# Top-k attention and two MLPs on one core: first head's keys and scores ahead of the rest, 64-token products with high and low words side by side, output chunks in pairs

## The chip, the cores and the metric

The kernel runs on one core of one Trainium2 chip. The metric is the device time in microseconds (us) of one execution, and the kernel's time is the median over its runs. One more execution is recorded by the hardware profiler; its span runs from the first instruction to the last. PE is TensorE (matmuls), PEld its weight loads, DVE VectorE, ACT ScalarE, POOL GpSimd, SP the engine that issues most DMAs.

## The reference, cut to what matters

```python
# q, k, v: 4 x 8 heads x 576 tokens x 64
scores = q @ k.T / sqrt(64)
kth    = the 32nd largest score of each row
attn   = softmax(scores where scores >= kth, else -1e9)
x      = (attn @ v), heads side by side           # 2304 tokens x 512
x      = (relu(x @ w_in) ** 2) @ w_out            # 512 -> 2048 -> 512
h      = x @ w2_in
out    = max(0.01 * h, h) @ w2_out
```

Everything is float32. The weights of the two MLPs reach the device as 64-bit words and are turned into two float32 parts there.

## The kernel before, in words

**Units and tiles.** The 2304 tokens are cut into nine units (`UNITS`: a batch, a first token, and 256, 320 or 64 tokens), and two heads form a head pair, so each unit has four. One head pair of one unit (a `uh` in the code) is cut into tiles of 128 rows of scores by 576 keys; the first tiles of the first `uh` belong to its first head, the next ones to its second. Two tiles form a pair. Only one unit has 64 tokens; its four head pairs make eight products of 64 tokens each.

**High and low words.** A float32 value is held as a rounded part (type float32r) and the remainder, so that a product becomes a few fast float32r products. `split_k` makes the two for one head's keys (the rounded part on ACT or POOL, the remainder on DVE for the first head pair), `split_q` for the queries. A score tile is made in two halves of 288 keys by `scores`: two matmuls, then an ACT copy to SBUF (L312).

**Top-k on DVE.** For each tile DVE runs four MAX8 (L929) and three MATCH_REPLACE8 (L931), written out slot by slot in the loop at the end; a pair of tiles has 16 slots. ACT then forms the exponentials, PE transposes them, and `av` or `av_split` multiplies with V. In `av_split` (L448) the transposed weights lie in `PTs` as four blocks of high words (0 to 3), four of low words (4 to 7) and one of leftover keys; nine matmuls of n columns add up in one PSUM bank. The two halves of the partitions are then added (ACT L453 copies one half, DVE L454 adds it to `xf`), and `x_out` splits the sum into `xh` (ACT L469) and `xl` (POOL L473). `xf` and `tmp` have one buffer each.

**MLP.** Token blocks of 512, 256, 384, 512, 256 and 384 go through the two MLPs as soon as their attention output is complete (`moe`, matmuls at L656, L693, L695). Each layer adds up in up to four PSUM banks (`acc`). After the second layer ACT copies each bank to an SBUF tile `y` (L714) and sends it out (L716). `y` is a 128 x 1024 tile of the tag `wc`, which has two buffers, and one chunk of 512 columns takes one such tile.

**What sets the order.** `at(slot, fn)` puts each step into a slot; the slots run in order, so the slot is a step's place in program order. Slots below zero lie ahead of the first MAX8. A scheduler then orders each engine's queue by that order and by planned times; `urgent` and `high_priority` move a step ahead in it, and `behind(key)` (`tc.issue_after`) places a step after a named instruction. `cur["rate"]` sets how many MLP pieces are put between the slots. Score tiles of the batches in `EARLY` are computed ahead by PE (slots 2 to 222) and stored in DRAM. On each engine the queue is worked in order.

Of the kernel before, what the change touches and what calls it, by code (L numbers as in the profile page):

```python
# [58 lines left out]
WCB = 2  # L59
# [29 lines left out]
def topk_attention_moe_moe2_kernel(  # L89
# [28 lines left out]
    def bank():  # L118
        return psum.tile([P, 512], F, tag="att", name="att", bufs=3)
# [4 lines left out]
    def behind(key):  # L124

        return tc.issue_after(cur[key].ins) if key in cur else ExitStack()

    def split_hi(dst, src, act=False):
        if act:
            ACT.activation(dst, src, AF.Copy)  # L130
            return
        POOL.tensor_scalar(dst, src, 1.0, 1.0, op0=OP.mult, op1=OP.mult)
# [84 lines left out]
    def at(slot, fn, *a):  # L217
        events.setdefault(slot, []).append((fn, a))
# [10 lines left out]
    def load_k(b, hp, st):  # L229
        if b in EARLY:  # L230
            KT[b, hp] = ahead.tile([P, 2, S], R, tag="KTa", name="KTa", bufs=KPB)
        else:
            KT[b, hp] = pool.tile([P, 2, S], R, tag="KT", name="KT", bufs=4)
        x = ahead if b in EARLY else pool
        st["k"] = x.tile([P, 2, S], F, tag="kraw", name="kraw", bufs=1 if b in EARLY else KRB)
        SP.dma_start(st["k"], k[b, hp])

    VT = {}
    vdram = {}
# [29 lines left out]

    def split_k(b, hp, st, h):  # L270
        raw, kt = st["k"][:, h], KT[b, hp][:, h]
        split_hi(kt, raw, st["i"] < 2)
        (DVE if (st["i"], h) in KLO_D else POOL).tensor_tensor(kt[64:128], raw[64:128], kt.bitcast(F)[64:128], op=OP.subtract)

    def load_q(uh):
# [6 lines left out]
    def split_q(uh, c):  # L282
        q1, q2 = uh["qs"]
        n = uh["n"]
        for h, o in ((0, W - 64 - n), (1, 64)):
            d1, d2, x = q1[:, h, o:o + n], q2[:, h, o:o + n], uh["q"][:, h, 0:n]
            if c == 0:
                split_hi(d1, x, uh["idx"] in HI_SET)
            else:
                (DVE if uh["idx"] in QLO_D else POOL).tensor_tensor(d2, x, d1.bitcast(F), op=OP.subtract)  # L290


    def scores(t, half):
        uh = t["uh"]
        d = uh["qs"]
        kt = KT[uh["b"], uh["hp"]]
        if half == 0:
            if direct(uh) and not kept(uh):
                t["s"] = sbufs[t["i"] % NS]
            else:  # L300
                t["s"] = ahead.tile([P, S], F, tag="stage", name="stage", bufs=NST)
        ks = slice(half * HALF, (half + 1) * HALF)
        mm = [(x[:, h, c:c + P], kt[:, h, ks]) for h, c in t["parts"] for x in d]
        if not direct(uh):
            ps = stage_psum.tile([P, 512], F, tag="sp", name="sp", bufs=SPB)
        elif t["i"] // 2 <= first_done + 1 or kept(uh):
            ps = stage_psum.tile([P, 512], F, tag="sd", name="sd", bufs=SDB)
        else:
            ps = bank()
        for i, (l, r) in enumerate(mm):  # L310
            PE.matmul(ps[:, 0:HALF], lhsT=l, rhs=r, start=i == 0, stop=i == len(mm) - 1)  # L311
        ACT.activation(t["s"][:, ks], ps[:, 0:HALF], AF.Copy, scale=0.125)  # L312
        if half == 1 and (kept(uh) or not direct(uh)):
            t["sd"] = dram.tile([P, S], F, tag=f"sd{t['i']}", name=f"sd{t['i']}")
            SP.dma_start(t["sd"], t["s"])
# [124 lines left out]
    def av_split(uh, h):  # L440
        n = uh["n"]
        c = slice(uh["c0"] + h * n, uh["c0"] + h * n + n)
        vt, pts = VT[uh["b"], uh["hp"]][0], late["PT"]
        ps = bank()[:, 0:n]
        mm = [(vt[:, h, j, :], pts[:, x + j, c]) for j in range(NJ) for x in (0, 4)]
        mm.append((vt[:, h, 4, :], pts[:, 8, c]))
        for i, (l, r) in enumerate(mm):
            PE.matmul(ps, lhsT=l, rhs=r, start=i == 0, stop=i == len(mm) - 1)  # L448
        if h == 0:
            uh["xf"] = late["pool"].tile([P, 320], F, tag="xf", name="xf", bufs=1)  # L450
            uh["tmp"] = late["pool"].tile([P, 320], F, tag="tmp", name="tmp", bufs=1)
        mine, other = slice(h * 64, h * 64 + 64), slice(64 - h * 64, 128 - h * 64)
        ACT.activation(uh["tmp"][mine, 0:n], ps[other], AF.Copy)  # L453
        DVE.tensor_tensor(uh["xf"][mine, 0:n], ps[mine], uh["tmp"][mine, 0:n], op=OP.add)  # L454

    def x_out(uh, hs):
        g0, n, hp = uh["u"]["g0"], uh["n"], uh["hp"]
# [169 lines left out]
    def moe(j, layer):  # L627
# [75 lines left out]
        for c in range(na):  # L703
            if layer == 0:
                xh, xl = x[c]
                with tc.high_priority(offset=SEAM):
                    ACT.activation(xh[:, 0:n], acc[c][:, 0:n], AF.Copy)
                    DVE.tensor_tensor(xl[:, 0:n], acc[c][:, 0:n], xh.bitcast(F)[:, 0:n], op=OP.subtract)
            else:
                if j == len(blocks) - 1:  # L710
                    y = sbufs[c][:, 0:512]
                else:
                    y = pool.tile([P, 1024], F, tag="wc", name="y", bufs=WCB)[:, 0:512]
                ACT.activation(y, acc[c], AF.Copy)  # L714
                for p0, n0, r0 in rows(blk["g0"] + c * P, P):
                    ACT.dma_start(out[r0:r0 + n0, :], y[p0:p0 + n0])  # L716
# [13 lines left out]
    for uh in in_time + [uh for uh in uhs if not direct(uh)]:  # L730
        b, hp, i = uh["b"], uh["hp"], uh.get("di")
        z = uh["zs"]
        if uh["first"] and direct(uh):
            st = {"i": i}
            st["n"] = len(order)
            order.append(b)
            z0 = after(z - 62, ("kraw", st["n"] - KRB), *[("KT", x, hp) for x in range(b)])
            at(z0, load_k, b, hp, st)
            for h in range(2):
                at(z0 + 12 * h + 11, split_k, b, hp, st, h)  # L740
            used["kraw", st["n"]] = z0 + 23
            assert z0 + 24 <= z
        if (b, hp) not in vdone or split(uh) and VTB < NHP:
            vdone.add((b, hp))
            zv = score_slot(uh["ti"]) + DLEAD + 4
            if split(uh):
                zv = max(zv, opened)
            at(zv, load_v, uh)
            if split(uh):
                at(zv + 6, split_v, uh, 0)  # L750
                at(zv + 9, split_v, uh, 1)
        if not direct(uh):
            continue
        uh["qs"] = qsets[i % 2]
        z0 = after(z - 70, ("qraw", i - 2))
        z1 = max(after(z - 20, ("q", i - 2)), z0 + 6)
        assert z1 + 4 <= z
        at(z0, load_q, uh)
        at(z1, split_q, uh, 0)
        at(z1 + 4, split_q, uh, 1)  # L760
        used["qraw", i] = z1 + 4
        used["q", i] = used["KT", b, hp] = (z if kept(uh) else score_slot(uh["last"])) + 2
# [48 lines left out]
    for p in range(NPAIRS):  # L811
        pr = dict(t=tiles[2 * p:2 * p + 2], p=p)
        pairs.append(pr)
        z = 16 * p
        if p == first_done:
            assert all(direct(t["uh"]) and not split(t["uh"]) for t in pr["t"])
            for i, t in enumerate(pr["t"]):
                at(z - DLEAD + 5 * i, scores, t, 0)
                at(z - DLEAD + 2 + 5 * i, scores, t, 1)
            at(z + 13, urgent(shifts), pr)  # L820
            for i in range(2):
                at(z + 13, urgent(drop), pr, i)
                at(z + 13, urgent(expo_sum), pr, i)
            at(z + 13, urgent(recip), pr)
            for i in range(2):
                at(z + 14, urgent(pt_main), pr["t"][i])
            at(z + 14, urgent(pt_left), pr)
            continue
        for i, t in enumerate(pr["t"]):
            if kept(t["uh"]):  # L830
                at(t["uh"]["zs"], scores, t, 0)
                at(t["uh"]["zs"] + 2, scores, t, 1)
            if kept(t["uh"]) or not direct(t["uh"]):
                at(z - LEAD + i, load_s, t)
            else:
                at(z - DLEAD + 5 * i, scores, t, 0)
                at(z - DLEAD + 2 + 5 * i, scores, t, 1)
            if i == 0:
                at(z + 14, shifts, pr)
            at(z + 14 + i, drop, pr, i)  # L840
            at(z + 16 + i, expo_sum, pr, i)
            if split(t["uh"]):
                at(z + 20 + i, norm, pr, i)
            at(max(z + 20 + 3 * i, z + 21 + i), pt_main, t)
        at(z + 18, recip, pr)
        at(z + 26, pt_left, pr)
# [160 lines left out]
```

## Time and profile before

| | |
|---|---|
| median of 3 runs | 1196.27 us (1195.66 to 1200.34) |
| profiled execution, its own time | 1196.31 us |
| its span | 1194.4 us |
| PE busy | 1126.8 us, 94% |
| DVE busy | 863.5 us, 72% |
| ACT busy | 804.7 us, 67% |
| POOL busy | 753.7 us, 63% |
| mean granted TensorE clock | 0.986 |

An engine's share is a mean over stages: DVE is nearly always busy while there is attention to do, up to about 900 us, and hardly afterwards; PE is busy nearly throughout from about 190 us on, when the first MLP begins.

### The profile page before, as it was taken

To read this page: it belongs to the slowest core of one execution; us is meant where nothing else is said; L and a number is where in the kernel's file an instruction comes from. 1 tells how busy PE (TensorE), PEld (TensorE's weight loads), DVE (VectorE), ACT (ScalarE), POOL (GpSimd) and SP (SyncE) were. 2 spreads that over 40 slices of the span, in tenths; PEclk is the share of its full clock that TensorE was granted. 3 is DMA by queue.
4 is the path that set the end of the run, shared out by engine and by line. 5 is a ranking of instruction groups with operands and counts; after the bars stand their busy time and mean duration, and the time that the engine had idled before them with its cause. 6 is when DMAs were issued, how large, how long until landed. Compare 5 with 4: busy or idle time off the path is not lost.

```text
span 1194.4 us, 20043 instructions
## 1 busy us (share of the span) xinstructions
PE 1126.8 (94%) x6376; PEld 987.6 (83%) x6376; DVE 863.5 (72%) x1797; ACT 804.7 (67%) x1785; POOL 753.7 (63%) x968
## 2 busy tenths in 40 slices
PE   5899978989899999899999999999999999999998
PEld 4777756768688889888999898788888899999997
DVE  7999998987878879999999999999991000110011
ACT  6999887998889878767777776766765233333322
POOL 7968747999878757867899675777755233002100
PEclk9899989999899999999999999999999999999999
DMA  9868766999899578899889888777665589779974
GB/s 313 273 213 292 242 229 233 333 356 329 296 311 316 211 234 297 298 360 392 300 315 323 276 303 273 266 228 219 212 211 159 170 317 346 252 249 346 358 251 135
DMA packets 108200, 329.53 MB, mean 276 GB/s; under 512 B 17216, under 2 KB 25408, under 8 KB 104000
## 3 DMA queue, kind: packets, MB, share of 16 engines
q1 hardware_dynamic: 105472, 323.53, 79.0%
q10 hardware_dynamic: 2624, 4.72, 1.1%
q8 instruction: 52, 0.85, 0.3%
q14 instruction: 52, 0.43, 0.1%
HBM read 257.03 MB, written 71.17 MB: 275 GB/s over the span
## 4 chain that ended last, share of the span: by engine, by line
PE 64%; DVE 6%; ACT 3%; POOL 3%; issue 1%; DMA 1%; ACTq 0%; POOLq 0%
PE h L656 28%; PE acc L695 15%; PE acc L693 13%; PE att L448 4%; DVE m L929 3%; PE att L351 3%; DVE w L931 2%; PE att L311 1%; DMA out_dram<-y 1%; POOL gl L676 1%; PE att L366 1%; ACT PTs L356 0%; POOL wo L568 0%; POOL wi L568 0%; ACT whole L358 0%
## 5 line engine op out<-in xcount | busy, mean ns | idle before, releaser
L656 PE MATMUL h<-xh,wi 128*128 128x512 f32 (+2 forms) x1280 | 345.0, 344 | 2.9 <-ACT ga L673 1.1
L929 DVE MAX8 m<-w 128x8 f32<-128x576 f32 x432 | 313.1, 748 | 2.6
L676 POOL TENSOR_TENSOR gl<-ga,gh 128x512 fp32r<-128x512 f32 (+2 forms) x160 | 163.2, 1022 | 143.4 <-ACT gh L675 116.5
L656 PEld LDWEIGHTS h<-xh,wi 128*128 128x128 f32 x1280 | 226.2, 190 | 27.7 <-ACT ga L666 2.1
L931 DVE MATCH_REPLACE8 w<-m,w 128x576 f32<-128x576 f32 x288 | 213.1, 742 | 0.7
L656 PE MATMUL h<-xl,wi 128*128 128x512 f32 (+2 forms) x640 | 204.5, 339 | 0.0
L359 POOL TENSOR_TENSOR PTs<-whole,PTs 128x512 fp32r<-128x512 f32 x112 | 145.4, 1303 | 42.6 <-ACT whole L358 42.2
L693 PE MATMUL acc<-gh,wo 128*128 128x512 f32 (+2 forms) x768 | 156.5, 342 | 4.9 <-ACT y L714 3.6
L695 PE MATMUL acc<-wo,gh 128*128 128x512 f32 x576 | 153.2, 397 | 2.0 <-ACT gh L675 2.0
L693 PEld LDWEIGHTS acc<-gh,wo 128*128 128x128 f32 x768 | 126.9, 190 | 18.0 <-ACT y L714 4.6
L330 ACT ACTIVATE e<-s,m 128x576 f32<-128x576 f32 x144 | 111.0, 784 | 26.0 <-DVE m L929 21.4
L656 PEld LDWEIGHTS h<-xl,wi 128*128 128x128 f32 x640 | 120.0, 189 | 10.2
L676 DVE TENSOR_TENSOR gl<-ga,gh 128x384 fp32r<-128x384 f32 x32 | 17.9, 559 | 151.2 <-ACT gh L675 150.7
L673 ACT ACTIVATE ga<-h 128x512 f32<-128x512 f32 (+2 forms) x96 | 46.5, 490 | 119.6 <-PE h L656 116.3
L695 PEld LDWEIGHTS acc<-wo,gh 128*128 128x128 f32 x576 | 105.5, 188 | 22.5 <-ACT gh L675 2.2
L929 DVE MAX8 m<-s 128x8 f32<-128x576 f32 x144 | 104.6, 747 | 20.5 <-ACT s L312 19.1
L334 ACT ACTIVATE e<-e,nb 128x576 f32<-128x576 f32 x144 | 111.6, 780 | 5.0 <-POOL nb L324 4.6
L931 DVE MATCH_REPLACE8 w<-m,s 128x576 f32<-128x576 f32 x144 | 106.6, 743 | 0.4
L351 PE MATMUL att<-ident,e 128*128 128x128 f32 x576 | 90.9, 279 | 7.8 <-ACT e L334 4.5
L693 PE MATMUL acc<-gl,wo 128*128 128x512 f32 (+2 forms) x384 | 88.7, 351 | 7.6 <-POOL gl L676 7.6
L346 POOL TENSOR_SCALAR e<-e,rc 128x576 f32<-128x576 f32 x112 | 83.7, 760 | 16.7 <-DVE rc L342 13.0
L668 POOL TENSOR_TENSOR ga<-ga 128x512 f32<-128x512 f32 (+2 forms) x80 | 67.0, 838 | 41.1 <-ACT gh L667 40.4
(100 smaller groups left out, 2080.7 us busy)
## 6 DMA issues: line engine op xcount, KB each, us to landing
wi<-wd SPq DMA_DIRECT2D x160, 512.0 KB, 5.5
wo<-wd SPq DMA_DIRECT2D x160, 512.0 KB, 5.3
wraw<-in_w_dram SPq DMA_DIRECT2D x32, 1024.0 KB, 7.5
sd<-stage SPq DMA_DIRECT2D x76, 288.0 KB, 3.0
s<-sd SPq DMA_DIRECT2D x76, 288.0 KB, 5.4
wd<-wi SPq DMA_DIRECT2D x32, 512.0 KB, 6.7
wd<-wo SPq DMA_DIRECT2D x32, 512.0 KB, 6.7
vd<-VT SPq DMA_DIRECT2D x16, 640.0 KB, 6.5
```

The lines of the kernel that those rows point to most:

```text
L330: ACT.activation(t["e"], t["s"], AF.Prelu, bias=pr["m8"][:, i, 31:32], scale=-1.0, alpha=1.0 / FAR)
L334: ACT.activation(e, e, AF.Exp, bias=pr["nb"][:, i:i + 1], scale=-FAR, accum_out=pr["sum"][:, i:i + 1])
L346: POOL.tensor_scalar(e, e, pr["rc"][:, i:i + 1], 1.0, op0=OP.mult, op1=OP.mult)
L351: PE.transpose(ps[:, j * P:(j + 1) * P], t["e"][:, j * P:(j + 1) * P], ident)
L359: POOL.tensor_tensor(pts[:, 4:8, c:c + P], whole, pts.bitcast(F)[:, 0:4, c:c + P], op=OP.subtract)
L656: PE.matmul(two[r][:, 0:n], lhsT=ws[r][:, w, c * P:(c + 1) * P], rhs=x[c][y][:, 0:n], start=cnt == mine[0], stop=cnt == mine[-1])
L668: POOL.tensor_tensor(a[:, 0:n], a[:, 0:n], a[:, 0:n], op=OP.mult)
L676: (DVE if j >= GLD else POOL).tensor_tensor(gl[:, 0:n], a[:, 0:n], gh.bitcast(F)[:, 0:n], op=OP.subtract)
L693: PE.matmul(acc[c][:, 0:n], lhsT=wo[:, w, cs], rhs=g[:, 0:n], start=first, stop=last)
L695: PE.matmul(acc[c], lhsT=g[:, cs], rhs=wo[:, w, :], start=first, stop=last)
L929: cur["dve"] = DVE.max(out=m8[:, x, 8 * r:8 * r + 8], in_=t["s"] if r == 0 else t["w"])
L931: cur["dve"] = DVE.match_replace(out=t["w"], in_to_replace=m8[:, x, 8 * r:8 * r + 8], in_values=t["s"] if r == 0 else t["w"], imm_value=NEG)
```

## The change

Five edits, with no change to the constants:

1. The keys of the first head pair are loaded in two halves: the first head's ahead of everything, then the first queries, then the second head's keys. The second head's split waits (`behind("opened")`) until the second score tile has been copied, and moves from slot -69 to slot -22.
2. The split of the second queries (`di == 1`) is also placed behind that copy.
3. The scores of the first pair of tiles are `urgent`.
4. A 64-token product takes a high and a low block together: the moving operand is 128 columns wide, there are four such matmuls and one of 64 columns in place of nine of 64. The copy and the add (L453, L454) become 128 wide, and a POOL add joins the two halves.
5. Two output chunks share one `wc` tile.

Since the raw keys have one buffer (`KRB = 1`), the later slot of the first head pair's last split also moves the loads of the following head pairs' keys to later slots (the second from -60 to -21).

```diff
-        SP.dma_start(st["k"], k[b, hp])
+        if st["i"]:
+            SP.dma_start(st["k"], k[b, hp])
+        else:
+            SP.dma_start(st["k"][:, 0], k[b, hp][:, 0])
+
+    def load_k_rest(b, hp, st):
+        SP.dma_start(st["k"][:, 1], k[b, hp][:, 1])
...
-        split_hi(kt, raw, st["i"] < 2)
+        with behind("opened") if st["i"] == 0 else ExitStack():
+            split_hi(kt, raw, st["i"] < 2)
...
-                split_hi(d1, x, uh["idx"] in HI_SET)
+                with behind("opened") if uh.get("di") == 1 else ExitStack():
+                    split_hi(d1, x, uh["idx"] in HI_SET)
...
-        ACT.activation(t["s"][:, ks], ps[:, 0:HALF], AF.Copy, scale=0.125)
+        out = ACT.activation(t["s"][:, ks], ps[:, 0:HALF], AF.Copy, scale=0.125)
+        if t["i"] == 1:
+            cur["opened"] = out
...
-        ps = bank()[:, 0:n]
-        mm = [(vt[:, h, j, :], pts[:, x + j, c]) for j in range(NJ) for x in (0, 4)]
+        m = 2 * n if n == 64 else n
+        ps = bank()[:, 0:m]
+        if n == 64:
+            mm = [(vt[:, h, j, :], pts[:, j:j + 5:4, c]) for j in range(NJ)]
+        else:
+            mm = [(vt[:, h, j, :], pts[:, x + j, c]) for j in range(NJ) for x in (0, 4)]
         mm.append((vt[:, h, 4, :], pts[:, 8, c]))
         for i, (l, r) in enumerate(mm):
-            PE.matmul(ps, lhsT=l, rhs=r, start=i == 0, stop=i == len(mm) - 1)
+            PE.matmul(ps[:, 0:n] if i == len(mm) - 1 else ps, lhsT=l, rhs=r, start=i == 0, stop=i == len(mm) - 1)
...
-        ACT.activation(uh["tmp"][mine, 0:n], ps[other], AF.Copy)
-        DVE.tensor_tensor(uh["xf"][mine, 0:n], ps[mine], uh["tmp"][mine, 0:n], op=OP.add)
+        xf, tmp = uh["xf"], uh["tmp"]
+        ACT.activation(tmp[mine, 0:m], ps[other], AF.Copy)
+        DVE.tensor_tensor(xf[mine, 0:m], ps[mine], tmp[mine, 0:m], op=OP.add)
+        if n == 64:
+            POOL.tensor_tensor(xf[mine, 0:n], xf[mine, 0:n], xf[mine, n:m], op=OP.add)
...
-                    y = pool.tile([P, 1024], F, tag="wc", name="y", bufs=WCB)[:, 0:512]
+                    if c % 2 == 0:
+                        both = pool.tile([P, 2, 512], F, tag="wc", name="y", bufs=WCB)
+                    y = both[:, c % 2]
...
             at(z0, load_k, b, hp, st)
+            if i == 0:
+                at(z0 + 6, load_k_rest, b, hp, st)
             for h in range(2):
-                at(z0 + 12 * h + 11, split_k, b, hp, st, h)
-            used["kraw", st["n"]] = z0 + 23
-            assert z0 + 24 <= z
+                at(-22 if i == 0 and h == 1 else z0 + 12 * h + 11, split_k, b, hp, st, h)
+            used["kraw", st["n"]] = -22 if i == 0 else z0 + 23
+            assert z0 + 23 <= z
...
-        at(z0, load_q, uh)
+        at(z0 if i else z0 + 12, load_q, uh)
...
-                at(z - DLEAD + 5 * i, scores, t, 0)
-                at(z - DLEAD + 2 + 5 * i, scores, t, 1)
+                mine = urgent(scores) if p == 0 else scores
+                at(z - DLEAD + 5 * i, mine, t, 0)
+                at(z - DLEAD + 2 + 5 * i, mine, t, 1)
```

## Rows read from the trace of the kernel before

**Rows 1.** Page, busy time of each engine: us, share of the span, instructions.
```profile
PE 1126.8 (94%) x6376; PEld 987.6 (83%) x6376; DVE 863.5 (72%) x1797; ACT 804.7 (67%) x1785; POOL 753.7 (63%) x968
```

**Rows 2.** Windows: stretch in us, its length, then each engine's busy time.
```profile
20.00:60.00 40.00, 33.71 (x190) 27.90 (x189) 40.00 (x87) 37.72 (x104) 34.87 (x51) 0.91 0.86 302
...
500.00:560.00 60.00, 57.88 (x406) 52.81 (x407) 59.13 (x134) 42.53 (x107) 44.45 (x68) 1.00 0.94 349
560.00:960.00 400.00, 395.96 (x2133) 348.55 (x2132) 336.46 (x729) 265.84 (x559) 280.74 (x348) 1.00 0.76 253
960.00:1194.00 234.00, 226.43 (x1382) 213.50 (x1380) 21.24 (x40) 72.55 (x159) 32.04 (x47) 0.99 0.82 283
```

**Rows 3.** Timeline of the opening: start, length, engine and line, operation.
```profile
0.74 0.65 SPq L280 DMA_DIRECT2D qraw<-in_q_dram  x1
1.45 0.58 SPq L236 DMA_DIRECT2D kraw<-in_k_dram  x1
...
3.88 0.72 ACT L130 ACTIVATE q<-qraw 128x256 fp32r<-128x256 f32 x2 [1.86 <-DMA qraw<-in_q_dram]
...
5.62 1.26 ACT L130 ACTIVATE KT<-kraw 128x576 fp32r<-128x576 f32 x2 [1.02 <-DMA kraw<-in_k_dram]
...
6.34 1.43 DVE L273 TENSOR_TENSOR KT<-kraw,KT 64x576 fp32r<-64x576 f32 x2 [1.25 <-ACT KT L130]
...
7.15 1.33 PE L311 MATMUL sd<-KT,q 128*128 128x288 f32 x4 [7.15 <-DVE KT L273]
...
9.02 0.76 DVE L929 MAX8 m<-s 128x8 f32<-128x576 f32 x1 [1.25 <-ACT s L312]
```

**Rows 4.** The chain that ended last, at 425 us: start, length, what.
```profile
425.34 6.60 DMA out_dram<-y
```

**Rows 5.** Waits: who waited for whom; us in total, times, longest (last: 950 to 1010).
```profile
ACT y L714 <- DMA out_dram<-y: 5.9, 2, 3.5
...
PE acc L693 <- ACT y L714: 3.6, 3, 2.0
...
PE acc L693 <- ACT y L714: 1.0, 1, 1.0
```

**Rows 6.** Timeline after 432 us, ACT and DVE; in brackets the idle time before.
```profile
432.46 0.77 ACT L334 ACTIVATE e<-e,nb 128x576 f32<-128x576 f32 x1
...
434.66 0.17 DVE L342 RECIPROCAL rc<-sum 128x2 f32<-128x2 f32 x1 [2.25 <-POOL sum L341]
```

**Rows 7.** The chain again, 489 to 565 us: first, one inside, last.
```profile
489.74 2.73 DVE m L929 x4
...
524.75 0.22 DVE xf L454
...
562.95 1.75 PE acc L695 x4
```

**Rows 8.** Timeline of PE: runs of products of 64 and of 256 columns.
```profile
516.23 2.20 PE L448 MATMUL att<-PTs,VT 128*128 128x64 f32 x19
...
528.06 0.28 PE L448 MATMUL att<-PTs,VT 128*128 128x64 f32 x1
...
550.43 1.11 PE L448 MATMUL att<-PTs,VT 128*128 128x256 f32 x8
```

**Rows 9.** Lines by shape on DVE: count, then us busy, mean ns, idle before.
```profile
L376 DVE TENSOR_TENSOR PTs<-att,PTs 64x128 fp32r<-64x128 f32 x16 | 4.5, 284 | 7.9 <-ACT PTs L375 7.4
L454 DVE TENSOR_TENSOR xf<-att,tmp 64x64 f32<-64x64 f32 x8 | 1.8, 220 | 0.2
```

**Rows 10.** Timeline of ACT and POOL after two of the 64-token products.
```profile
523.25 0.33 POOL L473 TENSOR_TENSOR xl<-xf,xh 128x64 fp32r<-128x64 f32 x1 [0.27 <-DVE m L929]
...
525.83 0.26 ACT L469 ACTIVATE xh<-xf 128x64 fp32r<-128x64 f32 x1
...
526.25 1.30 POOL L359 TENSOR_TENSOR PTs<-whole,PTs 128x512 fp32r<-128x512 f32 x1
527.50 0.33 POOL L473 TENSOR_TENSOR xl<-xf,xh 128x64 fp32r<-128x64 f32 x1
```

## Prediction

> **What bounds the kernel now.** I read the page of the profile first: PE is busy 94% of the span and DVE 72% [rows 1], but that is a mean over stages, so the second view is the windows [rows 2]. From 20 to 60 us DVE is busy 40.00 of 40 us and PE 33.71: the top-k on DVE sets the pace until the first MLP begins. From 500 to 560 us both are nearly full (DVE 59.13 of 60, PE 57.88), and from 560 us PE has 395.96 of 400 and then 226.43 of 234 us. So the end is set by DVE's start, then by DVE and PE taking turns, then by how much PE has left to do. The third view, the chain of waits, says where they take turns: it lies on DVE from 489.74 us to shortly before 562.95 us [rows 7], on PE after that, and it has one strange piece, an output DMA of 6.60 us at 425.34 us [rows 4].
>
> **The opening.** The first MAX8 starts at 9.02 us [rows 3]. It hangs on the keys: their load is issued second, at 1.45 us, brings 576 KB, and ACT begins its split at 5.62 us, while the 256 KB of queries issued at 0.74 us were in use at 3.88 us. So 576 KB took 5.62 - 3.88 = 1.74 us more, 331 KB a us. After the change 288 KB of keys come first: 3.88 us plus 32 KB at that rate, about 3.98 us. The queries follow 256 KB later, about 4.75 us. From ACT's start DVE's subtraction comes 0.72 us later (5.62 to 6.34) and the first matmul 0.81 us after that (6.34 to 7.15), so PE starts at about 5.51 us; the queries' split (0.36 us on ACT, about as much on DVE) is done by 5.8 us, in time for the second matmul. From the first matmul to the first MAX8 it is 9.02 - 7.15 = 1.87 us, hence 7.38 us, 1.64 us earlier. But the second head's subtraction, half of 1.43 us, today runs on DVE before the first MAX8, while DVE waits anyway; now it falls behind it, into a queue that has no idle time: +0.72 us. Net -0.9 us. Bounds: -1.6 us if the subtraction finds a gap, +0.7 us if the keys land no earlier. The extra DMA issue costs SP about 0.6 us, and the queries behind it are counted with that. The next head pair's keys wait for the same buffer and come later in program order; what hides that is the first pair's top-k, fourteen operations a tile pair of which the one at 9.02 us takes 0.76 us, on DVE. Without that cover the loss would be the keys' whole way, from issue to first MAX8 (9.02 - 1.45 = 7.6 us). The urgent scores and the second queries' split placed behind them I cost at nothing: ACT and PE have little to do in that stretch, and DVE sets the pace.
>
> **Output chunks in pairs.** Today chunk 2 takes the tile of chunk 0 and must wait for its output DMA. ACT stands still twice for that, 5.9 us in all, 3.5 the longest [rows 5]. With pairs, four chunks fill two tiles and nobody waits. PE waited 3.6 us in three places for such a copy; the 0.6 us that remain after 2.0 and 1.0 are a three-chunk block, where the copy was merely late. At 432 us I count the whole 2.0 us: ACT's queue is freed too, and behind the late copy stood the exponential at 432.46 us, for whose sum DVE idled 2.25 us at 434.66 us [rows 6], so DVE moves with PE. At 967 us PE has only MLP work left, and 1.0 us goes straight to the end. Together -3.0 us; bounds 0 (something else is late next) and -3.6.
>
> **64-token products.** Nineteen products of 64 columns take 2.20 us, one by itself 0.28, so (2.20 - 0.28) / 18 = 0.107 us from start to start. Eight of 256 columns take 1.11 us, (1.11 - 0.28) / 7 = 0.119 us [rows 8]. Four times the columns cost 11% more: the pace is set by something that each matmul pays, its weight load. A product of 128 columns lies between, so I take 0.11 us; each of the eight products loses four matmuls, 32 x 0.11 = 3.5 us of PE time. The Trainium skill (TensorE: Matmul & The Clock Gate, section Back-to-back issue gap) gives for a single matmul at the full clock a gap of its columns over 2.4 GHz plus 2.5 ns, which is 29 ns for 64 columns and 56 ns for 128; an estimate by that formula makes nine products 0.26 us and the new five 0.25 us, so the edit would be worth nothing. The trace disagrees, 0.107 us for 64 columns; the Trainium skill's section LDWEIGHTS on the same page, 107 ns for 128 columns of weights, is the one that agrees.
>
> These products lie around 516 and 528 us [rows 8], where the chain is DVE's. PE's time there is not lost, since its queue is filled with MLP work that can move up, but not all of it will: PE is 2.1 us idle from 500 to 560 us and DVE 0.9 [rows 2]. I count two thirds, -2.3 us. Against it: DVE's add becomes 128 wide. Its nearest rows are 284 ns for 64x128 and 220 ns for 64x64 [rows 9], so 8 x 0.064 = +0.5 us on the engine that leads. ACT's copy grows by as little, on an engine that is idle for 17 of these 60 us. POOL gets eight adds of about 0.33 us (the row at 523.25 us [rows 10], twice the partitions); what hides them is the room before the next unit's add: POOL is done with one head pair at 523.58 us, the next DVE add to the one buffer comes at 524.75 [rows 7], 1.2 us later. Net -1.8 us; bounds -3.5 and, with no PE gain and one POOL queue wait a unit, several us above zero (last rival).
>
> **Sum.** -0.9 - 3.0 - 1.8 = -5.7 us against the profiled execution's own 1196.31 us, which stands at the median of the runs (1196.27): 1190.6 us. A change within 0.5% (6.0 us, down to 1190.3) is about what a measurement of this kernel can tell from none, so the forecast lies at that edge.
>
> **The rivals.** *Everything is paid in full:* 1.6 + 3.6 + 3.5 = 8.7 us, 1187.6 us. For it speaks that PE is full to the end after 560 us; against it that DVE leads where the 64-token products lie.
>
> *Narrow products cost by the column.* If 64 columns take 0.107 us because they stream slowly and not because of the weights, 128 take 0.214, and 4 x 0.214 + 0.107 = 0.96 us is what nine cost now. Then only opening and chunks are left, less DVE's 0.5 us: 1196.3 - 0.9 - 3.0 + 0.5 = 1192.9 us. Against it: 256 columns at 0.119 us. The same end comes if the freed PE time is spent waiting for DVE. The Trainium skill's formula for a single matmul (TensorE: Matmul & The Clock Gate, section Back-to-back issue gap) would lead here too.
>
> *The POOL hop (slower than before).* The sum of a 64-token product now passes POOL, and ACT's `xh` stands behind it in ACT's queue. POOL can be in a long operation: `xh` ended at 526.09 us and its `xl` began at 527.50, behind a 1.30 us subtraction, 1.4 us late [rows 10]. If each of the eight hops takes 0.33 + 1.4 us and DVE, whose next add needs the same buffer, stands still with it, that is 13.8 us: 1196.3 - 0.9 - 3.0 + 0.5 + 13.8 = 1206.7 us. It decides from a hop of more than 1.2 us, the room computed above; that room and DVE's other work speak against it.
>
> **How the numbers follow.** My forecast, 1190.6 us with its own range 1188.6 to 1193, 0.48, nearly half of it below 1190.3. In full, 0.24, faster. By the column or lost to DVE, 0.17, within 0.5%. POOL hop, 0.11, slower. So faster 0.22 + 0.24 = 0.46, same 0.26 + 0.17 = 0.43, slower 0.11. The range: from the full payment with 1.6 us below it, 1186, to 1198, past the column case and into small losses, leaving out the full hop and the ends.
>
> **What would show it.** Right: first MAX8 near 7.4 us; no wait of `y` for an output DMA; 40 products in place of 72 at L448 for this unit, 0.11 us apart; PE's gaps at 432 and 967 us gone. Wrong: first MAX8 at 8.5 us or later; 128-column products 0.2 us apart; ACT or DVE idle before POOL's new add; the second head pair's scores late for DVE; or the scheduler's new order costing idle time in PE after 190 us in places the change does not touch.

## The result and the profile after

| | before | after |
|---|---|---|
| median of 9 runs each, in turn | 1196.84 us (1195.66 to 1200.34) | 1203.38 us (1199.92 to 1210.05) |
| ratio, with its 95% interval | | 1.0059 [1.0036, 1.0082] |
| profiled execution, its own time (span) | 1196.31 us (1194.4) | 1207.94 us (1206.2) |

The change made the kernel 6.5 us slower, where 1190.6 us and a range of 1186 to 1198 were forecast. The profiled execution of after lies in the upper part of its runs, so its trace overstates the loss: 11.6 us. Of all runs below one execution, of after at 218, is left out of its median: it took 1825.65 us at a granted clock of 0.56.

The page and the windows of after, for [rows 1] and [rows 2], with two stretches that turned out to matter (columns as there; after the busy times come the granted clock, the DMA share and GB/s):

```profile
PE 1129.2 (94%) x6344; PEld 988.7 (82%) x6344; DVE 863.4 (72%) x1797; ACT 804.3 (67%) x1785; POOL 755.9 (63%) x976
```

```profile
20.00:60.00 40.00, 31.93 (x178) 26.00 (x177) 39.85 (x87) 36.12 (x98) 33.47 (x48) 0.96 0.80 286
190.00:325.00 135.00, 117.71 (x525) 94.28 (x523) 113.21 (x210) 112.29 (x218) 119.01 (x119) 0.92 0.88 305
500.00:560.00 60.00, 53.45 (x355) 48.16 (x355) 59.07 (x133) 38.31 (x98) 45.91 (x76) 0.97 0.96 361
560.00:960.00 400.00, 392.05 (x2130) 344.09 (x2129) 344.94 (x748) 273.31 (x573) 283.86 (x353) 1.00 0.76 254
650.00:700.00 50.00, 45.42 (x263) 40.47 (x262) 49.53 (x107) 36.00 (x77) 38.06 (x50) 1.00 0.82 279
960.00:1194.00 234.00, 231.64 (x1411) 218.25 (x1410) 20.70 (x39) 72.98 (x160) 35.81 (x50) 1.00 0.83 290
```

The two new stretches in the kernel before:

```profile
190.00:325.00 135.00, 119.32 (x555) 95.43 (x555) 121.65 (x228) 119.36 (x231) 125.19 (x125) 0.96 0.92 326
650.00:700.00 50.00, 49.63 (x292) 45.40 (x292) 49.56 (x109) 37.67 (x83) 36.58 (x49) 1.00 0.88 291
```

32 matmuls are gone, as the change says, yet PE is busy 2.4 us longer and idle 9.4 us longer (1206.2 - 1129.2 against 1194.4 - 1126.8). From 650 to 700 us PE was full before and now stands still for 4.6 us. No edit touches what runs there. From 190 to 325 us PE did 30 matmuls and DVE 18 instructions fewer.

The opening of after, for [rows 3], and one row of DVE further on:

```profile
0.74 0.39 SPq L239 DMA_DIRECT2D kraw<-in_k_dram  x1
1.19 0.42 SPq L242 DMA_DIRECT2D kraw<-in_k_dram  x1
...
1.66 2.59 SPq L287 DMA_DIRECT2D qraw<-in_q_dram  x4
...
3.71 0.68 ACT L130 ACTIVATE KT<-kraw 128x576 fp32r<-128x576 f32 x1 [1.70 <-DMA kraw<-in_k_dram]
...
6.46 0.72 ACT L130 ACTIVATE q<-qraw 128x256 fp32r<-128x256 f32 x2 [2.07 <-DMA qraw<-in_q_dram]
...
8.80 0.76 DVE L951 MAX8 m<-s 128x8 f32<-128x576 f32 x1 [1.12 <-ACT s L320]
...
155.98 0.76 DVE L951 MAX8 m<-s 128x8 f32<-128x576 f32 x1 [4.02 <-ACT s L320]
```

The scheduler put the second head's keys (1.19) ahead of the queries (1.66), although their slot lies two behind the queries' slot. So the queries are in use at 6.46 us, not 4.75, and the first MAX8 comes 0.22 us earlier than before instead of 1.64. At 151.96 us DVE even runs dry for 4.02 us, since the scores of the next pair stood late in the queues of PE and ACT: from the 97th MAX8 to the 121st it was 35.1 us (131.4 to 166.5), before 29.2 us.

The paired chunks do what they should. ACT in after, where [rows 5] and [rows 6] had a wait of 3.5 us for an output DMA:

```profile
437.03 1.11 ACT L733 ACTIVATE y<-acc 128x512 f32<-128x512 f32 x2
...
437.98 0.65 ACT L733 ACTIVATE y<-acc 128x512 f32<-128x512 f32 x1
...
438.46 0.66 ACT L733 ACTIVATE y<-acc 128x512 f32<-128x512 f32 x1
```

### The profile page after: what moved, and what is told of

Read it like the earlier page. It is cut to its first block, busy times and chain, and to the rows that moved or that the text cites. A ratio compares the mean times of both kernels' runs of the same rounds, so it can differ in the third digit from the quotient of the medians.

```text
span 1206.2 us, 20003 instructions
## 1 busy us (share of the span) xinstructions
PE 1129.2 (94%) x6344; PEld 988.7 (82%) x6344; DVE 863.4 (72%) x1797; ACT 804.3 (67%) x1785; POOL 755.9 (63%) x976
## 4 chain that ended last, share of the span: by engine, by line
PE 66%; DVE 16%; ACT 9%; DMA 4%; issue 3%; POOL 1%; SPq 0%; ACTq 0%; POOLq 0%; DVEq 0%
PE h L673 26%; PE acc L712 15%; PE acc L710 10%; DVE m L951 8%; DVE w L953 6%; PE att L361 4%; PE att L462 3%; PE att L447 3%; PE sp L319 2%; DMA wraw<-in_w_dram 2%; ACT stage L320 1%; PE att L319 1%; ACT e L340 1%; ACT e L344 1%; ACT s L320 1%
```

## The experiments

"So many rows differ" compares the order of PE's matmuls in two traces, without line and buffer numbers. Runs of like matmuls count as one row; the kernel before has 2,381 rows, and those differ that are not in the longest order common to both.

### The edits apart

Edits 1 to 3 alone, that is after with the old `av_split` and the old chunks:

```diff
-            mm = [(vt[:, h, j, :], pts[:, j:j + 5:4, c]) for j in range(NJ)]
...
-            POOL.tensor_tensor(xf[mine, 0:n], xf[mine, 0:n], xf[mine, n:m], op=OP.add)
...
-                    y = both[:, c % 2]
+                    y = pool.tile([P, 1024], F, tag="wc", name="y", bufs=WCB)[:, 0:512]
```

> Edits 1 to 3 alone (the opening). In the changed kernel the first block's attention ended 0.5 us earlier than before (last xh of the block at 189.4 against 189.9 us), but the first MLP phase, from there to its seam, ended 11.8 us later (325.6 against 313.8). Theory A: the opening's new order of the queues does this, in a stretch where the code of the change does nothing itself; then this kernel loses the same 8 to 12 us by the first seam and ends 5 to 11 us slower than before. Theory B (the POOL add and the wider product cost it): this kernel is within 2 us of before. Theory C (any new order costs about as much): this one and the next three are all 3 to 8 us slower.

Edit 4 alone, in the kernel before:

```diff
+            mm = [(vt[:, h, j, :], pts[:, j:j + 5:4, c]) for j in range(NJ)]
...
+            POOL.tensor_tensor(xf[mine, 0:n], xf[mine, 0:n], xf[mine, n:m], op=OP.add)
```

> Edit 4 alone (64-token products). Its queues are those of before up to about 500 us. Theory A: 0 to 3 us faster, products 0.11 us apart. Theory B: 5 us or more slower, lost between 505 and 560 us. Theory C: 3 to 8 us slower, at no one place.

Edit 5 alone, in the kernel before:

```diff
-                    y = pool.tile([P, 1024], F, tag="wc", name="y", bufs=WCB)[:, 0:512]
+                    if c % 2 == 0:
+                        both = pool.tile([P, 2, 512], F, tag="wc", name="y", bufs=WCB)
+                    y = both[:, c % 2]
```

> Edit 5 alone (output chunks in pairs). Its queues are those of before up to the first output copies at 425 us. Theory A: 2 to 3 us faster, the two waits of the copy for the output DMA gone. Theory B: the same as A. Theory C: 3 to 8 us slower.

Edits 4 and 5 together, the last two diffs in one kernel:

> Edits 4 and 5 without the opening. Theory A: 2 to 6 us faster than before, that is about 1190 to 1194 us, and 9 to 12 us faster than the changed kernel. Theory B: as slow as the changed kernel, near 1203 us. Theory C: 3 to 8 us slower than before.

Measured against 1196.94 us: edits 1 to 3 1216.26 us, 1.0148 [1.0126, 1.0171]; edit 4 1198.11, 1.0011 [1.0002, 1.0020]; edit 5 1194.88, 0.9986 [0.9971, 1.0001]; edits 4 and 5 1199.48, 1.0022 [1.0014, 1.0031]. The parts don't add up to the whole (+19.3, +1.2 and -2.1 us against +6.5). What they share is that PE keeps the order of before only up to a point: for three rows with edits 1 to 3 (218 rows differ), to 506 us with edit 4 (166 rows), to 434 us with edit 5 (156 rows) and with edits 4 and 5 (173 rows). That raised the question what a new order costs when no work is changed at all.

### A neutral constant, loads alone, scores first, no POOL hop

`FILL` is the stretch of slots over which the early score tiles are spread. Moving its end changes no instruction, only places in the order: the traces of the kernel before at the four constants used below hold the same operations on every engine and move the same 329.53 MB. In the kernel before:

```diff
-FILL = (2, 222)
+FILL = (2, 223)
```

> The kernel before with one constant changed: the early score tiles of batches 2 and 3 are spread over slots 2 to 223 and not 222. No work is added, removed or made cheaper, but the queues of all engines come out in another order from about 60 us on. Theory C (the order itself is the cost; any new order moves the time by some us): the first seam moves by 3 us or more from 313.8 us, and the time by 3 us or more from 1196.9. Theory A (the opening's own edits do the harm): within 2 us of before in both.

The loads of edit 1 alone, in the kernel before:

```diff
+            SP.dma_start(st["k"][:, 0], k[b, hp][:, 0])
...
+                at(z0 + 6, load_k_rest, b, hp, st)
...
-        at(z0, load_q, uh)
+        at(z0 if i else z0 + 12, load_q, uh)
```

> Of the opening only the loads: first head's keys, then the first queries, then the second head's keys; the splits, the later key loads and the queries' split stand as before. Theory A with the late split as the cause: first MAX8 about as before (the queries still come in third place on the queue, 8.8 to 9.2 us), first seam within 3 us of 313.8, time within 3 us of before. Theory C: seam and time off by as much as the opening's 11 us, one way or the other, since the order changes from the first instruction on.

In after, the scores of all pairs up to the one that closes the first attention block made urgent:

```diff
-                at(z - DLEAD + 5 * i, scores, t, 0)
-                at(z - DLEAD + 2 + 5 * i, scores, t, 1)
+                at(z - DLEAD + 5 * i, urgent(scores), t, 0)
+                at(z - DLEAD + 2 + 5 * i, urgent(scores), t, 1)
...
-                mine = urgent(scores) if p == 0 else scores
+                mine = urgent(scores) if p <= first_done else scores
```

> The changed kernel with one more edit: the scores of all pairs up to the one that closes the first block are urgent, not only those of the first. In the changed kernel DVE idles 4.0 us at 152 us for scores that stand behind early score tiles in PE's and ACT's queues, and the subtraction that releases the first weights runs at 180.2 us, before 171.7. Theory A (this starving is what costs the 12 us): no such idle time, the subtraction near 172 us, the first seam near 314 us, time 1190 to 1197. If the starving is not what costs: the subtraction earlier, the seam still near 325, time near 1203.

Edits 4 and 5 without the POOL hop:

```diff
-            POOL.tensor_tensor(xf[mine, 0:n], xf[mine, 0:n], xf[mine, n:m], op=OP.add)
+            DVE.tensor_tensor(xf[mine, 0:n], xf[mine, 0:n], xf[mine, n:m], op=OP.add)
```

> Edits 4 and 5 without the opening, with the second add of the 64-token products on DVE and not on POOL. With it on POOL, POOL stood still 2.6 us for DVE's first add, and PE waited 3.6 us for V's split behind it; 1199.5 us. If the POOL hop is what makes edit 4 lose: 4 us or more faster, 1193 to 1195.5, that wait gone. If the order is: anything from 1194 to 1201, and waits of the same size in other places.

Measured against 1198.56 us: neutral constant 1207.78, 1.0084 [1.0067, 1.0101]; loads alone 1210.86, 1.0112 [1.0094, 1.0130]; scores first 1206.08, 1.0062 [1.0043, 1.0080]; no POOL hop 1203.66, 1.0050 [1.0034, 1.0067]. The neutral constant alone costs as much as the whole change, or more. Making the late scores urgent too took little of DVE's starving away: it still waited 2.4 us at 155.62 us, and its 121st MAX8 came at 165.9 us (166.5 in after), so this run doesn't tell what the starving costs. Without the POOL hop the kernel is slower than with it (1.0050 against 1.0022); its order is another one too and DVE has eight adds more, so this doesn't price the hop. Its order is that of before up to 434 us, so an order kept that long is no safeguard either.

### Neutral constants on both kernels, and the load order as predicted

The end of `FILL` at 216, 218, 223 and 226, in the kernel before (223 was run above) and in after, for example:

```diff
-FILL = (2, 222)
+FILL = (2, 216)
```

> The changed kernel with the end of the early-scores stretch one slot later (FILL from (2, 222) to (2, 223)); the same work. Theory A (the loss is that of a re-planned order, and the constants fit only the order of the kernel before): a neutral constant moves this kernel too, by 3 us or more in either direction from its 1203.4 us; anything from 1195 to 1210 us. Rival B (the five edits themselves cost 6.5 us, in waits that they add): it stays within 2.5 us of 1203.4 us.

> The changed kernel with FILL (2, 216), six slots earlier; the same work. Theory A: again a time of its own between 1195 and 1212 us, with the first seam of the MLP (first matmul of the second block) moved by several us from 325.6 us. Rival B: 1203.4 us within 2.5 us.

> The kernel before with FILL (2, 216) and no edit at all: the same work, another order. Theory A: 1201 to 1212 us, as the other neutral constant gave 1207.8 us, with PE busy 150 to 153 us in the stretch from 500 to 660 us against 155.3 us. Rival B, and the case that (2, 223) was merely a bad constant: 1194 to 1200 us.

> The kernel before with FILL (2, 218), no edit. If its fitted order is an exception: 1202 to 1212 us, as the other two neutral constants. If these were bad draws: 1192 to 1200 us.

> The kernel before with FILL (2, 226), no edit. Fitted order an exception: 1202 to 1212 us. Bad draws: 1192 to 1200 us.

> The changed kernel with FILL (2, 218). If the edits save the 5.7 us that were forecast, only between orders that were not fitted: 1198 to 1206 us, and the mean of the changed kernel's orders 4 to 7 us below the mean of those of the kernel before. If the edits are worth nothing or cost time: as far up as the kernel before at this constant, or further.

> The changed kernel with FILL (2, 226). Edits save their part: 1198 to 1206 us. Edits worth nothing: 1205 to 1211 us.

Medians, with the ratio to the kernel before run beside each:

```
end of FILL       before                            after
222 (as given)    1196.84                           1203.38  1.0059 [1.0036, 1.0082]
223               1207.78  1.0084 [1.0067, 1.0101]  1203.82  1.0055 [1.0038, 1.0071]
216               1209.26  1.0099 [1.0084, 1.0114]  1201.50  1.0035 [1.0022, 1.0049]
218               1207.17  1.0076 [1.0051, 1.0101]  1207.39  1.0079 [1.0056, 1.0101]
226               1203.88  1.0054 [1.0034, 1.0073]  1203.55  1.0047 [1.0031, 1.0063]
```

All four neutral constants make the kernel before slower, by 5.4 to 9.9 parts in a thousand; its own order is the exception. For after, 222 is one constant among others: the five lie from 1201.5 to 1207.4 us. At the four other constants the means of the ratios are 1.0078 for before and 1.0054 for after: the edits save 2.4 parts in a thousand, 2.9 us. But the four differences are -2.9, -6.4, +0.3 and -0.7 parts, so whether the edits save anything between such orders is not settled. The expectation that the means lie 4 to 7 us apart was too high.

In after, the second head's keys behind the first queries:

```diff
-        SP.dma_start(st["k"][:, 1], k[b, hp][:, 1])
+        with behind("firstq"):
+            SP.dma_start(st["k"][:, 1], k[b, hp][:, 1])
...
-                at(z0 + 6, load_k_rest, b, hp, st)
+                at(z0 + 14, load_k_rest, b, hp, st)
```

> The changed kernel with the second head's keys issued behind the first queries (a step placed after the queries' load), as the prediction assumed. By the prediction's opening term the first MAX8 starts at 7.4 to 7.7 us in place of 8.80 us, whatever comes after. For the whole, theory A: the 287 lines of PE's queue that move decide, anything from 1195 to 1212 us; the theory that the late queries are what the loss comes from: 1.2 us less than the changed kernel, about 1202 us.

The time is 1202.2 us, 1.0040 [1.0021, 1.0058], and the first MAX8 comes at 8.05 us; 7.4 to 7.7 had been expected. Its opening:

```profile
0.74 0.39 SPq L239 DMA_DIRECT2D kraw<-in_k_dram  x1
1.18 0.65 SPq L288 DMA_DIRECT2D qraw<-in_q_dram  x1
1.89 0.58 SPq L243 DMA_DIRECT2D kraw<-in_k_dram  x1
2.51 1.86 SPq L288 DMA_DIRECT2D qraw<-in_q_dram  x3
3.59 0.68 ACT L130 ACTIVATE KT<-kraw 128x576 fp32r<-128x576 f32 x1 [1.58 <-DMA kraw<-in_k_dram]
...
5.72 0.72 ACT L130 ACTIVATE q<-qraw 128x256 fp32r<-128x256 f32 x2 [1.45 <-DMA qraw<-in_q_dram]
...
8.05 0.76 DVE L954 MAX8 m<-s 128x8 f32<-128x576 f32 x1 [1.13 <-ACT s L323]
```

Even in the right order the queries are in use 4.54 us after their issue (5.72 - 1.18); issued first they took 3.88 - 0.74 = 3.14 us [rows 3]. Both had loads issued behind them; what is new is the load ahead.

This run also says something about the late scores: DVE's 121st MAX8 came at 160.2 us (158.7 before, 166.5 in after), and the time is still 4.7 us above the kernel before. DVE is 1.5 us late at that point; the order loses more than that.

### The control, and the version that beats both

The kernel before, and the kernel with edit 5 alone, each with

```diff
-FILL = (2, 222)
+FILL = (2, 221)
```

At this end every engine's queue holds the same instructions in the same order as at 222; the two traces of the kernel before agree row by row on every engine.

> Control: the kernel before with FILL (2, 221). The constant differs as in the other neutral constants, but here every engine's queue holds the same instructions in the same order as before. If the order is what costs: no difference, 1196 to 1200 us, ratio within 0.2% of 1. If something else about the constant costs: 1203 us or more.

> Edit 5 (paired chunks) alone, with FILL (2, 221): every queue as in the run of edit 5 alone, 1194.88 us against 1196.94. If the order is what costs and the edit gives back about 2 us: 1193 to 1197 us, ratio 0.996 to 1.000; if the earlier 2 us were chance, ratio 0.999 to 1.002.

Measured against 1197.68 us: the control 1197.40, 0.9997 [0.9986, 1.0009]; edit 5 in the order of edit 5 alone 1194.65, 0.9976 [0.9966, 0.9985]. So a constant costs nothing by itself: the order does. And edit 5 alone is faster than both kernels, by 3.0 us than before and by 8.7 us than after's median in the first comparison.

## Where the time went

The next table counts what work PE has left. Each matmul counts the median pitch of its kind over these runs (the time from its start to the next one's), whatever the clock, and the remaining work of the kernel before at the same moment is taken off. A number that rises says that PE did less useful work in that stretch than before; kernels with edit 4 begin 3.8 us lower, since the 32 matmuls are not to be done. The control shows how far two executions of one order can lie apart here: it lost 3.0 us between 150 and 250 us, and from column to column 0.7 at most after that.

```
us into the run         0   150   250   350   410   440   560   660   700   900
control (221)         0.0  -0.1   2.9   2.2   2.3   2.1   2.1   1.8   2.0   2.2
edit 5 (221)          0.0   0.0   0.2   0.0   0.5  -2.9  -1.3  -3.2  -3.3  -2.3
edit 4               -3.8  -3.3  -3.1  -3.4  -2.9  -3.1   0.8   1.3   1.7   2.0
before, 223           0.0  -0.2   3.4   3.0   3.3   3.2   3.3   3.5   9.7  11.9
before, 216           0.0   1.9   5.2   6.3   7.0   5.2   6.7   5.9  13.7  12.6
before, 218           0.0   1.2  -2.1   0.5   0.9   1.8   2.8   2.2   8.0   9.1
before, 226           0.0  -0.6  -2.0  -1.4  -1.2  -1.1   1.2   1.3   5.7   6.1
after                -3.8  -0.3   3.7   8.5   8.6   4.3   7.7   6.2  12.3  11.9
after, 216           -3.8  -0.1   2.6   0.6   0.6  -3.3  -0.7   1.5   3.2   5.4
after, 226           -3.8  -1.6  -2.9  -1.1  -0.6  -4.3  -2.1   1.0   2.1   5.2
```

Read by columns, three things stand out. From 410 to 440 us every kernel with edit 5 gains 3.4 to 4.3 us. From 440 to 560 us the kernels with edit 4 lose 2.2 to 3.9 us, those without 0 to 2.3; the clean case is edit 4 alone, in the order of before up to 506 us: it loses 3.9 us, all that its narrower products save. From 500 to 560 us its PE was busy 55.87 us (before 57.88, control 56.18) at a granted clock of 0.97 (1.00 in both), so part of this is idle time and part the clock. And from 660 to 700 us, at the change from the first to the second MLP of the third block (384 tokens), all four neutral orders of before lose 4.4 to 7.8 us and after 6.1 (its other orders 1.7, 1.1 and, at 223, not in the table, 3.3), with no work changed there; the control loses 0.2. On top, after lost 8.8 us between 150 and 350 us. With the same edits it lost 0.7 there at 216, 0.5 at 226 and 6.0 at 223, so the edits as such don't cost that.

The windows at that change in the kernel before, in its own order (two lines) and with 223 (three), then PE's timeline with 223 (idle before and its releaser in brackets):

```profile
660.00:670.00 10.00, 9.69 (x61) 8.88 (x60) 9.87 (x22) 6.85 (x18) 9.15 (x12) 1.00 0.87 300
670.00:680.00 10.00, 10.00 (x56) 9.02 (x55) 9.93 (x23) 6.23 (x14) 6.37 (x8) 1.00 0.74 228
```

```profile
650.00:660.00 10.00, 7.70 (x53) 7.31 (x51) 9.87 (x22) 6.93 (x15) 9.84 (x14) 1.00 0.78 252
660.00:670.00 10.00, 7.31 (x32) 5.05 (x32) 9.91 (x22) 7.55 (x17) 7.72 (x11) 0.78 0.72 270
670.00:680.00 10.00, 10.00 (x56) 9.52 (x56) 8.83 (x20) 5.38 (x12) 5.20 (x8) 0.88 0.43 139
```

```profile
659.59 1.21 PE L448 MATMUL att<-PTs,VT 128*128 128x256 f32 x8 [2.30 <-POOL PTs L359]
...
663.17 1.38 PE L351 MATMUL att<-ident,e 128*128 128x128 f32 x8 [1.25 <-POOL e L346]
...
665.79 1.01 PE L656 MATMUL h<-xh,wi 128*128 128x384 f32 x2 [0.52 <-ACT xh L707]
...
668.39 1.49 PE L656 MATMUL h<-xh,wi 128*128 128x384 f32 x4
...
676.96 0.86 PE L656 MATMUL h<-xh,wi 128*128 128x384 f32 x4
```

The kernel before passes the same place with one wait of 0.31 us, and after with a string of short ones:

```profile
663.82 0.44 PE L656 MATMUL h<-xh,wi 128*128 128x384 f32 x1 [0.31 <-ACT ga L673]
```

```profile
661.24 0.39 PE L462 MATMUL att<-PTs,VT 128*128 128x256 f32 x1 [0.96 <-ACT whole L368]
662.52 0.97 PE L710 MATMUL acc<-gl,wo 128*128 128x384 f32 x4 [0.90 <-POOL gl L693]
...
669.01 0.62 PE L673 MATMUL h<-xh,wi 128*128 128x384 f32 x2 [1.17 <-ACT xh L724]
670.31 0.96 PE L673 MATMUL h<-xh,wi 128*128 128x384 f32 x4 [0.69 <-DVE xl L725]
```

PE can't begin the second MLP before ACT (L707) and DVE (L708) have split the first one's output. In the kernel before, ACT's four copies come as soon as PE is done, and the first step of the next exponentials (L330) stands behind them:

```profile
656.03 1.64 ACT L707 ACTIVATE xh<-acc 128x384 fp32r<-128x384 f32 x4 [0.47 <-PE acc L693]
657.57 1.50 ACT L330 ACTIVATE e<-s,m 128x576 f32<-128x576 f32 x2
```

With 223 two of these steps stand ahead of the copies in ACT's queue, and each waits for DVE's top-k first:

```profile
660.04 0.78 ACT L330 ACTIVATE e<-s,m 128x576 f32<-128x576 f32 x1 [2.66 <-DVE m L929]
662.15 0.77 ACT L330 ACTIVATE e<-s,m 128x576 f32<-128x576 f32 x1 [1.34 <-DVE m L929]
...
664.11 0.49 ACT L707 ACTIVATE xh<-acc 128x384 fp32r<-128x384 f32 x1
```

From the start of the first MLP's last matmul to the first copy it is 2.5 us there, 4.4 us at 216, 1.9 at 218 and 3.4 at 226, each time with two such steps ahead; in the kernel before and in the control the copy comes 0.2 us before that matmul. In after one such step stands ahead of the first copy and one ahead of the other three. So the traces name the place: what stands in front of these copies in ACT's queue. It is not that DVE was late: at 226, by the same count for DVE, DVE was 1.4 us ahead of the kernel before at 660 us, and PE lost 4.4 us all the same. How much of the loss hangs on this one place was not tried by moving it alone; attention products that waited for POOL, as in the rows with 223, add to it.

The earlier loss of after is read from its chain of waits between 195 and 250 us, of which 52.5% lie on the load of the raw MLP weights; three of its pieces:

```profile
201.71 8.84 DMA wraw<-in_w_dram
...
214.23 9.88 DMA wraw<-in_w_dram
...
230.11 10.16 DMA wraw<-in_w_dram
```

These loads start when a conversion step has freed their buffer, and ACT's conversion steps stand between exponentials and scores in its queue; in after the top-k step behind which the first converted weights are placed (the subtraction at L334, L324 before) runs at 180.2 us instead of 171.7, and the first of these steps after it comes at 185.1 instead of 176.3. That the 8.8 us come from there was argued from the chain, not tried by itself.

## Why the prediction was wrong

**The step that failed** is the sum itself: "-0.9 - 3.0 - 1.8 = -5.7 us against the profiled execution's own 1196.31 us". It takes for granted that every instruction which the edits don't touch stays where it was. It did not: 225 of PE's 2,381 rows differ between the two kernels, and each of the four other orders of the kernel before (165 to 199 rows) costs 5.4 to 9.9 parts in a thousand, 6 to 12 us, with no work changed. There was no term and no rival for that; it was named only in the last sentence on what would make the prediction wrong. That after's 6.5 us are the price of its order, and not of its edits, is concluded from this comparison: at those four constants the edits make the kernel no slower on average. The terms by themselves:

**Opening, -0.9 us: mis-sized, then lost.** The first half of the keys was in use at 3.71 us (predicted 3.98), but the queries at 6.46 (predicted 4.75), because the scheduler issued the second half first; with the order as assumed, at 5.72, and even there the gain was used up by the 25th MAX8 (37.5 us, as before). In after the first MAX8 moved by 0.22 us, the 25th was 1.1 us later than before (38.6 against 37.5) and the 121st 7.8 us (166.5 against 158.7). "The urgent scores and the second queries' split placed behind them I cost at nothing" covered steps that reorder the queues from the start.

**Chunks, -3.0 us: right in mechanism and sum, not in its parts.** No wait for an output DMA is left, and edit 5 alone measured -2.1 us, then -3.0. By the count of the table all of it came at 432 us, 3.4 us from 410 to 440, and only 0.3 from 960 to 1020, where 1.0 was forecast: other waits of PE, 2.5 us from 950 to 1010, took the place of 1.2 us. Its order is that of before up to 434 us, which may be why the gain shows at all.

**64-token products, -1.8 us: the pace right, the share wrong.** The 128-column products start 0.11 us apart in edit 4 alone (511.83, 511.94, 512.06, 512.17 us); the group of five is one row there:

```profile
511.77 0.64 PE L452 MATMUL att<-PTs,VT 128*128 128x128 f32 x5
```

So the column rival's price was wrong, and 3.8 us of PE work did go. By the formula of the Trainium skill (TensorE: Matmul & The Clock Gate, section LDWEIGHTS) a weight load of 128 columns is estimated at 107 ns; the starts in the trace agree with that, 0.11 us apart at 128 moving columns as well as at 64. But "two thirds" was a choice between bounds, and the other end came true: DVE is busy 59 of 60 us there, as before, and PE had no less work left at 560 us than in the kernel before (0.8 us more, by the table). Its waits from 500 to 560 us in edit 4 alone are put down to POOL (3.6 us) and ACT (1.1), none to DVE itself; that the stretch still goes at DVE's pace is argued. Edit 4 alone measured +1.2 us.

**The POOL hop** that would have cost 13.8 us did not: the adds take 0.32 us each, and in after ACT waited for them 1.9 us in three places, 0.9 the longest, while DVE was busy 59.07 of 60 us. The hop has a price that the prediction did not look for: POOL stood still 3.5 us in three places before these adds, until DVE had made its own. What that cost was not measured. The forecast of that rival, 1206.7 us, lies close to what was measured, for another reason.

## What to carry to other kernels

When a scheduler orders the queues, price an edit against the spread of orders as well as against the trace: change a constant that alters no work, see how far the time moves, and only then believe a term of a few microseconds. A kernel can stand on a lucky order, as this one does: each of the four other orders tried is slower. Every edit here that moves the first instructions throws it away. One that leaves the order alone until late may keep its gain (the paired chunks did) or not (edit 4 did not, nor edits 4 and 5). A comparison of the orders tells beforehand how early an edit cuts in; compare edits that cut in early over several constants, not at one.

## What the runs showed of the hardware that was not expected

A wait of PE can cost twice. In the kernel before with 223 PE paused several times from 657 to 668 us; the granted clock was 0.78 from 660 to 670 us and 0.88 from 670 to 680 (stretches at 2.4 and at 1.2 GHz together), where it is 1.00 in the kernel before, and four 384-column matmuls took 1.49 us at 668.39 against 0.86 at 676.96 when the clock was back. The other neutral orders show the same there: 0.97 and 0.69 at 216, 0.71 and 0.95 at 218, 0.66 and 1.00 at 226. In after it stayed at 1.00, with PE busy only 6.21 of the first 10 us, in shorter pauses. Over a whole run the clock does not tell the orders apart: 0.978 and PE busy 1133.7 us with 223, 0.980 and 1133.6 us in the control, 0.986 and 1126.8 us in the kernel before, each with the same 6,376 matmuls.

A load takes longer with others ahead of it: 256 KB of queries took 3.14 us from issue to use when issued first, 4.54 us as the second of several and 6.46 - 1.66 = 4.80 us as the third. What stretches them, a shared rate or something else, no run varied by itself. A rate worked out from two loads, as in the prediction, fitted the first load and not the second.
